# Layer 1 folds along d by a half turn; filter rows by plain loads from SP instead of indirect ones from POOL

## The chip, the cores and the metric

The kernel runs on one core of a Trainium2 chip. The metric is the device time of one execution in microseconds (us). Engines are named as the profile names them: PE (matmuls), PEld (its weight loads), DVE, ACT, POOL, SP. SP, ACT and POOL issue DMAs, which 16 DMA engines carry out.

## What is computed

Four blocks on x of 2048 rows (s) by 448 columns (d), bf16: a spectral filter, an FFN, and both again with the same weights.

```python
def _A_ref(x, w_r, w_i):                       # spectral filter
    X = rfft2(x.astype(float32), axes=(-2, -1))
    X = X * (w_r + 1j * w_i)                   # filter W: 2048 x 225
    return irfft2(X, s=(S, D)).astype(bfloat16)

def _B_ref(x, w1, b1, w2, b2):                 # FFN, 448 -> 1792 -> 448
    r = relu(x @ w1 + b1)
    return (r * r) @ w2 + b2

x = x + _A_ref(_layernorm(x), A_w_r, A_w_i)
x = x + _B_ref(_layernorm(x), B_w1, B_b1, B_w2, B_b2)
x = x + _A_ref(_layernorm(x), A_w_r, A_w_i)
x = x + _B_ref(_layernorm(x), B_w1, B_b1, B_w2, B_b2)
```

## The kernel before

Row s = 16p + t of x lies on partition p, tile t, so x is 16 tiles of 128 x 448. The Fourier transform along s is split into a part over p (128 points, matmuls with the matrix FA) and a part over t (16 points, matrices G and G0); the transform along d is the matrix TD. In layer 1 the stages follow each other like this.

*First stage (`first_A`, line 890).* For each tile t: mean and standard deviation (`ln_stats` on DVE, or `act_stats` on ACT for tiles 1, 3 and 5), their reciprocal (line 885), then `scaled` (lines 756 to 764) multiplies FA by it into `Fs`. Five matmuls per tile use x as the stationary operand and Fs as the moving one. They fold d as they go: the sum and the difference of x at d and at 447 - d come out, which are the cosine and the sine half. The mirrored upper half must lie in memory in mirrored order, so nine copies `XR` (lines 836 to 840) write it into `xr`, a view of `VT`. The fifth matmul takes off the mean. The result is copied out of PSUM into `XA`.

*TD (`stage_TD`, line 924).* 16 steps of four matmuls, each 224 columns, and the copy out (`TD_out`) into `U`. Layer 2 folds twice and uses `TQ` with eight smaller matmuls per pair of steps and a copy that interleaves even and odd frequencies.

*B, W, Bi (lines 952 to 1010).* B does the 16-point transform with G; the result goes to `EF`. `stage_W` (line 981, the operation at line 984, recorded at line 778) multiplies by the filter on DVE: one multiply per n, 128 partitions x 896 elements, which reads through `W_at` (line 797) column block n of the first two blocks of `Wt` and column block 15 - n of the last two. `stage_Bi` brings the product back with H. Then TI and FI (lines 1012 and 1034) finish the inverse transform, and the FFN follows.

*The filter rows in `Wt`.* Partition 32j + 16r + k holds 16 consecutive rows of the filter, 7200 bytes, twice (r = 0, 1). Blocks 0 and 1 are the real and the imaginary part of rows 128k + 16j + 1 and on, blocks 2 and 3 those of the rows counted from the end. Four indirect DMAs on POOL (`gather`, line 825) fetch them with the index table `ix`. Row 0 takes the place of one row that does not exist; two small loads on SP (line 1338) write it over the gathered data, and wait for it.

*Order and waits.* The program is a list of operations with their dependences. `_pages` names the memory pieces that an operation reads and writes. `_Sched.schedule` places the operations in the order of five lists written out by hand, `ORDER`, one for each engine; its times are a model which decides about waits' positions, PSUM banks and the warm-up matmuls on `ones` (line 1364) that fill gaps of PE. Each engine runs its list in order, and an operation that waits holds up all that stand behind it. DMAs of SP go out in the list's order too. In the list of before, SP issues x (alternating with ACT), FA third, `ix`, TD, G, G0, then H (which waits for a reciprocal of the first stage, line 1335), row 0 of the filter, TI, FI, J, biases, W1, TQ, W2.

Of the kernel before, what the change touches and what calls it, by code (L numbers as in the profile page):

```python
# [9 lines left out]
U32 = mybir.dt.uint32  # L10

P = 128
S = 2048
# [20 lines left out]
def make_constants():  # L34
# [21 lines left out]
    l = np.arange(1, 225)[None, :]  # L56
    th = 2 * np.pi * l * (dd - 223.5) / D
    TD = np.zeros((2, 2, P, LW))
    for g, M in enumerate((np.cos(th), -np.sin(th))):
        TD[g, 0] = M[:P]  # L60
        TD[g, 1, 32:] = M[P:]
# [58 lines left out]
    p = np.arange(P)  # L120
    j, k = p // 32, p % 16
    ix = np.stack([P * k + 16 * j + 1, P * (16 - k) - 16 * j - 16], 1)


# [8 lines left out]
    return dict(FA=np.concatenate([FA, -FA], 1), FI=np.concatenate([FI, -FI], 1), TD=TD, G=G, H=H, G0=G0, TI=TI, TQ=TQ, ix=ix,  # L133
# [17 lines left out]
1270 1275 1236 1242 1280 1283 1286 1289 1292""",  # L151
    "act": """
# [11 lines left out]
1035 1172 1184 1177 1174 1179 1182 1253 1246 1248 1251 1256 1261 1268 1278 1266 1263 1271 1258 1273 1276""",  # L164
    "dve": """
# [22 lines left out]
1281 1243 1287 1290 1293""",  # L188
    "pool": """
16 24 25 17 41 23 27 29 81 26 28 22 30 104 21 31 20 32 143 146 18 19""",  # L190
    "sp": """
3 5 6 8 9 11 13 15 33 34 35 150 151 152 153 154 155 156 157 158 159 160 161 162 163 281 301 319 322 321 339 357 375
393 943 964 982 984 985 1002 1020 1038 1150 1056 1147 1188 1144 1194 1241 1191 1235 1285 1238 1141 1282 1244 1288 1197
1291 1294""",
# [10 lines left out]
HALVES = True  # L205
LATE = (4, 4)
# [71 lines left out]
def _pages(ap):  # L278

    if isinstance(ap, _PsAP):  # L280
        return [ap.tile]
    pat = list(ap.ap)
    row = pat[0][0]
    name = ap.tensor.name
    off = np.array([ap.offset % row if row else ap.offset])
    for step, cnt in pat[1:]:
        off = (off[:, None] + step * np.arange(cnt)[None, :]).reshape(-1)
    pg = np.unique(off * mybir.dt.size(ap.dtype) // 4)
    return [(name, int(i)) for i in pg]


class _Sched:
# [6 lines left out]
    DMA_FIRST = 3500.0  # L299
# [76 lines left out]
    def schedule(self):  # L376
# [55 lines left out]
        def ready_of(u):  # L432
            if u not in ready:
                r, off = 0.0, 0.0
                for op in u.ops:
                    for d in op.gdeps:
                        if d.unit is not u:
                            same = d.eng == u.eng and not d.is_dma
                            r = max(r, done[d] + d.lat + (40.0 if u.eng == "pe" else 0.0) - off)
                    off += op.cost  # L440
                ready[u] = r
            return ready[u]
# [34 lines left out]
        while total:  # L477
# [83 lines left out]
            for op in u.ops:  # L561
# [3 lines left out]
                if op.is_dma:  # L565
                    dma_free = max(dma_free, t + 1800.0) + op.lat
                    done[op] = dma_free
# [54 lines left out]
def bass_interleave_layers__spectral_gfnet__dense_activation_squared_relu__prompt_kernel(nc, A_x, A_w_r, A_w_i, B_x, B_w1, B_b1, B_w2, B_b2, out):  # L622
# [3 lines left out]
    dc = {k: nc.inline_tensor(_bf16_round(v), name=f"c_{k}").ap().bitcast(BF16) for k, v in cst.items() if k != "ix"}  # L626
# [829 lines left out]
```

## Time and profile before

| | us |
|---|---|
| median of 3 runs (lowest, highest) | 256.54 (256.44, 257.36) |
| span of the profiled execution | 254.8 |
| PE busy in the span | 246.0 (97%) |
| DVE, ACT, POOL busy | 193.3, 166.5, 12.5 |

One execution was profiled; its span runs from the first to the last instruction, and the median time is 1.7 us longer. Matmuls are pipelined, so a busy PE is not PE at its peak. The page has the span in 40 slices of 6.37 us, busy shares in tenths (9 is 90% or more), the clock granted to TensorE in tenths of full speed, the busy share of the DMA engines, and GB/s:

```profile
PE   6899979999999999999999999999999999999996
DVE  2995988889872899997999998999993078320543
ACT  5896988994287894026847898999449783006600
POOL 3880000000000000000000000000000000000000
PEclk9999999999999999999999999999999999999999
DMA  6999954212111000130000000021223001142004
GB/s 191 380 329 379 293 154 131 42 43 45 36 41 44 0 4 0 41 42 3 0 3 1 3 3 3 3 41 45 46 77 40 0 3 27 37 92 73 3 0 145
```

The DMA engines are busy for the first five or six slices and nearly idle afterwards; POOL works in the first three only.

### The profile page before, as it was taken

The page shows a single profiled execution, that of the slowest core. Times are in us where ns is not written, and L with a number is a line of the kernel's source. Part 1 is how long each engine was busy: PE and PEld are TensorE (multiplying, and loading weights), DVE is VectorE, ACT ScalarE, POOL GpSimd, SP SyncE. Part 2 cuts the span into 40 slices and gives each one's busy share as a digit, 9 for nine tenths or more (in the row PEclk, how much of TensorE's full clock was granted, in tenths as well). Part 3 has the DMA queues.
Part 4 walks back from the last instruction along what each step waited for, and adds up shares of the span by engine and source line. Part 5 has one row for each costly group of instructions (what it writes and reads, how often), then busy time and mean ns, then how long its engine had stood idle before and what let it go on. Part 6 is the DMA issues. An engine that isn't in the chain of part 4 may idle for free.

```text
span 254.8 us, 6150 instructions
## 1 busy us (share of the span) xinstructions
PE 246.0 (97%) x2462; PEld 153.9 (60%) x2462; DVE 193.3 (76%) x628; ACT 166.5 (65%) x362; POOL 12.5 (5%) x26
## 2 busy tenths in 40 slices
PE   6899979999999999999999999999999999999996
PEld 2578777886544555554566688798544445545454
DVE  2995988889872899997999998999993078320543
ACT  5896988994287894026847898999449783006600
POOL 3880000000000000000000000000000000000000
PEclk9999999999999999999999999999999999999999
DMA  6999954212111000130000000021223001142004
GB/s 191 380 329 379 293 154 131 42 43 45 36 41 44 0 4 0 41 42 3 0 3 1 3 3 3 3 41 45 46 77 40 0 3 27 37 92 73 3 0 145
DMA packets 24080, 18.10 MB, mean 71 GB/s; under 512 B 16082, under 2 KB 22706, under 8 KB 24052
## 3 DMA queue, kind: packets, MB, share of 16 engines
q1 hardware_dynamic: 22756, 13.22, 19.3%
q0 software_dynamic: 576, 3.69, 3.9%
q10 hardware_dynamic: 720, 0.80, 1.0%
q8 instruction: 19, 0.31, 0.5%
q14 instruction: 9, 0.07, 0.1%
HBM read 12.20 MB, written 1.84 MB: 55 GB/s over the span
## 4 chain that ended last, share of the span: by engine, by line
PE 82%; ACT 7%; DVE 4%; DMA 2%; issue 1%; POOL 1%; SPq 0%; DVEq 0%; POOLq 0%
PE ps L724 82%; ACT arena L749 4%; ACT VT L749 2%; DMA FA_sb<-c_FA 2%; ACT wide L749 1%; DVE st L854 1%; DVE Fs L761 1%; DVE XA L750 1%; PE ps L1364 0%; POOL Wt L827 0%; DVE x_sb L1217 0%; POOL Fs L761 0%; SPq L716 0%; POOL VT L750 0%; DVE VT L750 0%
## 5 line engine op out<-in xcount | busy, mean ns | idle before, releaser
L724 PE MATMUL ps<-wide,W_sb 64*128 64x512 bf16 (+1 forms) x770 | 90.0, 347 | 0.0
L724 PE MATMUL ps<-W_sb,arena 128*128 128x448 bf16 (+3 forms) x476 | 86.8, 342 | 0.0
L724 PEld LDWEIGHTS ps<-wide,W_sb 64*128 64x128 bf16 (+1 forms) x770 | 51.3, 95 | 36.1 <-issue 0.7
L743 ACT ACTIVATE arena<-ps,b1col 128x512 bf16<-128x512 f32 x84 | 51.9, 690 | 28.9 <-PE ps L724 28.6
L724 PEld LDWEIGHTS ps<-W_sb,arena 128*128 128x128 bf16 x476 | 45.5, 98 | 38.1 <-issue 0.4
L778 DVE TENSOR_TENSOR arena<-arena 128x512 bf16<-128x512 bf16 (+1 forms) x140 | 44.2, 367 | 29.6 <-ACT arena L743 29.5
L1095 ACT ACTIVATE VT<-x_sb 128x448 bf16<-128x448 bf16 x28 | 16.1, 581 | 13.3 <-DVE x_sb L1071 13.2
L749 ACT ACTIVATE arena<-ps 128x896 bf16<-128x896 f32 (+1 forms) x27 | 20.6, 854 | 3.1 <-PE ps L724 3.1
L743 ACT ACTIVATE mv<-mv,epst 128x1 f32<-128x1 f32 (+1 forms) x45 | 12.8, 297 | 11.8 <-DVE mv L855 8.4
L743 ACT ACTIVATE arena<-ps 128x256 bf16<-128x256 f32 x56 | 17.8, 399 | 0.9 <-PE ps L724 0.7
L778 DVE TENSOR_TENSOR wide<-arena,Wt 128x896 bf16<-128x896 bf16 x32 | 17.8, 623 | 0.4 <-DMA Wt<-in_A_w_r_dram,ix 0.3
L749 ACT ACTIVATE XA<-ps 128x512 bf16<-128x512 f32 (+1 forms) x28 | 15.3, 595 | 3.2 <-PE ps L724 3.2
L724 PE MATMUL ps<-H_sb,wide 64*128 64x128 bf16 x512 | 15.7, 217 | 1.5 <-issue 1.4
L1217 DVE SCALAR_TENSOR_TENSOR x_sb<-ps,mv,xin 128x448 bf16<-128x448 f32 (+2 forms) x13 | 8.0, 644 | 11.7 <-PE ps L724 11.5
L724 PEld LDWEIGHTS ps<-H_sb,wide 64*128 64x128 bf16 x512 | 14.4, 94 | 3.5 <-issue 1.5
L724 PE MATMUL ps<-wide,VT 64*128 64x512 bf16 x42 | 15.8, 377 | 0.0
L749 ACT ACTIVATE wide<-ps 128x896 bf16<-128x896 f32 (+3 forms) x20 | 14.1, 761 | 2.2 <-PE ps L724 2.1
L749 ACT ACTIVATE VT<-ps 128x512 bf16<-128x512 f32 (+1 forms) x16 | 12.5, 857 | 1.2 <-PE ps L724 1.2
L1364 PE MATMUL ps<-ones 128*128 128x512 bf16 (+2 forms) x32 | 9.6, 420 | 2.6 <-DVE mv L855 1.0
L760 ACT ACTIVATE wide<-x_sb,rstd 128x448 bf16<-128x448 bf16 x12 | 7.8, 664 | 6.3 <-DVE mv L787 6.0
L750 DVE CAST arena<-ps 128x448 bf16<-128x448 f32 (+1 forms) x11 | 8.8, 832 | 3.1 <-PE ps L724 3.1
L1071 DVE SCALAR_TENSOR_TENSOR x_sb<-ps,mv,xin 128x448 bf16<-128x448 f32 x16 | 10.4, 680 | 0.8 <-PE ps L724 0.7
(79 smaller groups left out, 275.1 us busy)
## 6 DMA issues: line engine op xcount, KB each, us to landing
out_dram<-x_sb SPq DMA_DIRECT2D x15, 112.0 KB, 1.8
W_sb<-in_B_w_dram SPq DMA_DIRECT2D x1, 1568.0 KB, 7.5
H_sb<-c_H SPq DMA_DIRECT2D x2, 768.0 KB, 9.9
W_sb<-in_B_w_dram SPq DMA_DIRECT2D x1, 1344.0 KB, 10.8
xin<-in_A_x_dram SPq DMA_DIRECT2D x3, 224.0 KB, 5.2
G_sb<-c_G SPq DMA_DIRECT2D x1, 512.0 KB, 6.0
xin<-in_A_x_dram ACTq DMA_DIRECT2D x2, 224.0 KB, 4.8
VT<-in_B_w_dram SPq DMA_DIRECT2D x2, 192.0 KB, 3.1
```

Of the source, the lines that this page charges most:

```text
L724: return sch.add("pe", lambda e: e.matmul(_res(o), lhsT, rhs, start=start, stop=stop, skip_group_check=skip), [lhsT, rhs], [o], cost=cost, ...
L743: sch.add("act", lambda e: e.activation(o, _res(i), func, **kw), rd, [o], cost=c)
L749: op = sch.add(engs[0], lambda e: e.activation(o, _res(i), ACT.Copy) if h[0].eng == "act" else e.tensor_copy(o, _res(i)), [i], [o], cost=c ...
L750: e.tensor_copy(o, _res(i)), [i], [o], cost=c[engs[0]], unit=unit)
L760: op = sch.add(engs[0], lambda e: e.activation(o, i, ACT.Copy, scale=s) if h[0].eng == "act" else e.tensor_scalar(o, i, s, 1.0, op0=ALU.mu ...
L761: e.tensor_scalar(o, i, s, 1.0, op0=ALU.mult, op1=ALU.mult), [i, s], [o], cost=c[engs[0]])
L778: sch.add(eng, lambda e: e.tensor_tensor(o, _res(a), b, op), [a, b], [o], cost=_free(o) / rate + 69.0)
L854: small(lambda e, si=si, xi=xi: e.bn_stats(si, xi), [xi], [si], _free(xi) / 0.96 + 69.0)
L1071: small(lambda e, xx=xx, xi=xi, r=r, m=m: e.scalar_tensor_tensor(out=xx, in0=_res(r), scalar=m, in1=xi, op0=ALU.subtract, op1=ALU.add), [r ...
L1095: op = sch.add("act", lambda e, i=i, o=o, x=x, h=h: e.activation(o, x, ACT.Square, accum_out=sd[:, i, 1:2]) if h[0].eng == "act" else e.sc ...
L1217: small(lambda e: e.scalar_tensor_tensor(out=o, in0=_res(i), scalar=rs[0] if rs else 1.0, in1=xi, op0=ALU.add if t >= 4 and last else ALU. ...
L1364: return lambda e: e.matmul(ps[:, b, 0:n], ones[:], ones[:, None, :].to_broadcast([P, n // P, P]), start=True, stop=True)
```

## The change

Layer 1 now folds along d by a half turn: the sum and the difference of x at d and at d + 224 come out of the first stage. They are the even and the odd frequencies, and each needs cosine and sine, so TD holds both for half of the frequencies. The upper half is read where it lies, and the mirrored copies are gone. TD's matmuls write even and odd frequencies into separate columns of PSUM, and the copy out interleaves them, as in layer 2.

The filter rows come by 16 plain loads on SP, one for each of four blocks and each j: 32 partitions, a source access pattern with a count of 2 at stride 0 outermost, then 16 rows, then 3600 elements. In the last block of partitions of blocks 2 and 3 the load leaves out the first row's place, so that the loads of row 0 touch other bytes. `_pages` tells the quarters of `Wt`'s partitions apart.

FA is the first DMA on ACT's queue; x's tiles 1, 3 and 5 follow there, all other tiles go on SP. H no longer waits for the first stage and stands behind row 0 of the filter. The planner's model of a DMA's time and its price of a scaling on DVE are changed, and the five lists of `ORDER` are new: in them POOL has 14 of the first stage's 16 scalings, before 5.

```diff
-    for g, M in enumerate((np.cos(th), -np.sin(th))):
+    for g in range(2):
+        th = 2 * np.pi * np.arange(2 - g, 226 - g, 2)[None, :] * (dd - 223.5) / D
+        M = np.concatenate([np.cos(th), -np.sin(th)], 1)
         TD[g, 0] = M[:P]
         TD[g, 1, 32:] = M[P:]
...
+XLOADS = ((0, 1, "sp"), (1, 1, "act"), (2, 1, "sp"), (3, 1, "act"), (4, 1, "sp"), (5, 1, "act"), (6, 2, "sp"), (8, 2, "sp"),
+          (10, 2, "sp"), (12, 2, "sp"), (14, 2, "sp"))
...
+    if name == "Wt":
+        p = ap.offset // row
+        return [(name, int(i), q) for q in range(p // 32, (p + pat[0][1] - 1) // 32 + 1) for i in pg]
...
-        for a, n, q in ((0, 1, "sp"), (1, 1, "act"), (2, 1, "sp"), (3, 1, "act"), (4, 1, "sp"), (5, 1, "act"), (6, 2, "sp"),
-                        (8, 2, "act"), (10, 2, "sp"), (12, 2, "act"), (14, 2, "sp")):
+        dma("act", FA_sb[:], dc["FA"])
+        for a, n, q in XLOADS:
             dma(q, xin[:, a:a + n, :], x_dram[:, a:a + n, :])
-            if a == 2:
-                dma("sp", FA_sb[:], dc["FA"])
-            if a == 4:
-                dma("sp", ix[:], dc["ix"])
...
-        def gather(c, w, a, n):
-            o = Wt[:, a:a + n * (LW + 1)]
-            sch.add("pool", lambda e: e.indirect_dma_start(o, None, (A_w_r, A_w_i)[w], bass.IndirectOffsetOnAxis(ix[:, c:c + 1], 0)),
-                    [ix[:, c:c + 1]], [o], is_dma=True, cost=1150.0, lat=160.0 * n)
-
-        sch.bias, sch.tag = PR["M"], "M"
-        for w in range(2):
-            gather(0, w, WS * w, 16)
-        sch.tag = "M2"
-        for w in range(2):
-            gather(1, w, WS * (2 + w), 16)
-        for a in range(0, NT, 2):
-            for b in range(a, a + 2) if a == 0 else (a,):
-                n = 1 if a == 0 else 2
-                sch.bias, sch.tag = PR["A1"] - PR["A1step"] * a / 2, f"XR.{b}"
-                evac(xr[:, b:b + n, :], xin[:, b:b + n, D - 1:HD - 1:-1], EV["XR"])
+        def rows(c, w, j):
+
+            a, R, o = (A_w_r, A_w_i)[w], LW + 1, WS * (2 * c + w)
+            d = R + 1 if c == 1 and j == 3 else 0
+            k = (S - 16 - 16 * j if c else 16 * j + 1) * R + d
+            dma("sp", Wt[32 * j:32 * j + 32, o + d:o + WS],
+                bass.AP(a.tensor, a.offset + k, [[0, 2], [-P * R if c else P * R, 16], [1, WS - d]]))
+
         sch.bias, sch.tag = 0.0, ""
         dma("sp", TD_sb[:], dc["TD"])
-        dma("sp", G_sb[:], dc["G"])
-        dma("sp", G0_sb[:], dc["G0"])
+        for c in range(2):
+            for w in range(2):
+                for j in range(4):
+                    sch.tag = f"M.{c}.{w}.{j}"
+                    rows(c, w, j)
+            sch.tag = ""
+            if c == 0:
+                dma("sp", G_sb[:], dc["G"])
+                dma("sp", G0_sb[:], dc["G0"])
...
-                    mm(o(k), xr[:, t, D0[k]:D0[k] + P], F1, False, False, skip=True, unit=u)
+                    mm(o(k), xin[:, t, HD + D0[k]:HD + D0[k] + P], F1, False, False, skip=True, unit=u)
...
                         if first:
-                            l0, w, m = g * LW, LW, TD_sb[:, g, k, :]
+                            r, m = 1 - g, TD_sb[:, g, k, :].rearrange("p (q i) -> p q i", q=2)
+                            o = t[lambda b, i=i, r=r: ps[:, b + i, :].rearrange("p (q w) -> p q w", q=2)[:, :, r * QD:(r + 1) * QD]]
...
-        for i in range(2):
-            dma("sp", H_sb[:, 8 * i:8 * i + 8], dc["H"][:, 8 * i:8 * i + 8], after=[rstd[:, 10 + 2 * i, 0:1]])
         for w, a in enumerate((A_w_r, A_w_i)):
             sch.tag = f"L.W0.{w}"
             dma("sp", Wt[96:128, WS * (2 + w):WS * (2 + w) + LW + 1],
                 bass.AP(a.tensor, a.offset, [[0, 2], [P * (LW + 1), 16], [1, LW + 1]]))
         sch.tag = ""
+        for i in range(2):
+            dma("sp", H_sb[:, 8 * i:8 * i + 8], dc["H"][:, 8 * i:8 * i + 8])
```

More of the change, by code (lines that the diff above doesn't have):

```diff
@@ L9 @@
 FP32 = mybir.dt.float32
-U32 = mybir.dt.uint32
 P = 128
@@ L55, in make_constants @@
     dd = np.arange(HD)[:, None]
-    l = np.arange(1, 225)[None, :]
-    th = 2 * np.pi * l * (dd - 223.5) / D
     TD = np.zeros((2, 2, P, LW))
-    for g, M in enumerate((np.cos(th), -np.sin(th))):
+    for g in range(2):
+        th = 2 * np.pi * np.arange(2 - g, 226 - g, 2)[None, :] * (dd - 223.5) / D
+        M = np.concatenate([np.cos(th), -np.sin(th)], 1)
         TD[g, 0] = M[:P]
@@ L117, in make_constants @@
     H = H.reshape(P, 16, 2, 3, 64)
-    p = np.arange(P)
-    j, k = p // 32, p % 16
-    ix = np.stack([P * k + 16 * j + 1, P * (16 - k) - 16 * j - 16], 1)
     l0 = np.arange(1, 225)[:, None]
@@ L131, in make_constants @@
             TI[:, r, g] = M[r::2]
-    return dict(FA=np.concatenate([FA, -FA], 1), FI=np.concatenate([FI, -FI], 1), TD=TD, G=G, H=H, G0=G0, TI=TI, TQ=TQ, ix=ix,
+    return dict(FA=np.concatenate([FA, -FA], 1), FI=np.concatenate([FI, -FI], 1), TD=TD, G=G, H=H, G0=G0, TI=TI, TQ=TQ,
                 J=np.eye(P)[::-1])
@@ L141 @@
     "pe": """
[9 rows of a table removed]
-1270 1275 1236 1242 1280 1283 1286 1289 1292""",
-    "act": """
[11 rows of a table removed]
-1035 1172 1184 1177 1174 1179 1182 1253 1246 1248 1251 1256 1261 1268 1278 1266 1263 1271 1258 1273 1276""",
-    "dve": """
[22 rows of a table removed]
-1281 1243 1287 1290 1293""",
[9 rows of a table added]
+1267 1272 1277 1244 1238 1285 1288 1282 1291 1294""",
+    "act": """
[11 rows of a table added]
+1174 1186 1181 1184 1176 1055 1248 1255 1253 1250 1258 1260 1268 1263 1280 1278 1273 1270 1275 1265""",
+    "dve": """
[22 rows of a table added]
+1283 1292 1295""",
     "pool": """
-16 24 25 17 41 23 27 29 81 26 28 22 30 104 21 31 20 32 143 146 18 19""",
+15 59 51 43 93 96 75 67 83 109 18 119 122 145 135 132 17 16""",
     "sp": """
-3 5 6 8 9 11 13 15 33 34 35 150 151 152 153 154 155 156 157 158 159 160 161 162 163 281 301 319 322 321 339 357 375
-393 943 964 982 984 985 1002 1020 1038 1150 1056 1147 1188 1144 1194 1241 1191 1235 1285 1238 1141 1282 1244 1288 1197
-1291 1294""",
+4 6 8 10 11 12 13 14 19 20 21 22 23 24 25 26 27 28 29 30 31 32 33 34 35 36 37 152 153 154 155 156 157 158 159 160
+161 162 163 164 165 283 303 321 324 323 341 359 377 395 945 966 984 986 987 1143 1004 1146 1149 1022 1152 1040 1237
+1243 1193 1058 1196 1199 1190 1240 1287 1284 1246 1290 1293 1296""",
 }
@@ L298 @@
     NDSEM = {"sp": 40, "pool": 8, "act": 5, "pe": 0, "dve": 0}
-    DMA_FIRST = 3500.0
+    DMA_FIRST = 2000.0
+    LAND = 400.0
     TURN = 100.0
@@ L438, in ready_of @@
                             same = d.eng == u.eng and not d.is_dma
-                            r = max(r, done[d] + d.lat + (40.0 if u.eng == "pe" else 0.0) - off)
+                            r = max(r, done[d] + (60.0 if d.is_dma and d.cost != 1000.0 else d.lat) + (40.0 if u.eng == "pe" else 0.0) - off)
                     off += op.cost
@@ L565, in schedule @@
                 if op.is_dma:
-                    dma_free = max(dma_free, t + 1800.0) + op.lat
-                    done[op] = dma_free
+                    if op.cost == 1000.0:
+                        dma_free = done[op] = max(dma_free, t + 1800.0) + op.lat
+                    else:
+                        begin = max(dma_free, t + (450.0 if e == "pool" else 1100.0))
+                        dma_free = begin + op.lat * (1.1 if begin < 3400.0 else 2.0 if begin < 5000.0 else 1.08)
+                        done[op] = dma_free + self.LAND
                 for w in op.takes:
@@ L625, in bass_interleave_layers__spectral_gfnet__dense_activation_squared_relu__prompt_kernel @@
     cst = make_constants()
-    dc = {k: nc.inline_tensor(_bf16_round(v), name=f"c_{k}").ap().bitcast(BF16) for k, v in cst.items() if k != "ix"}
-    dc["ix"] = nc.inline_tensor(cst["ix"].astype(np.uint32), name="c_ix").ap()
+    dc = {k: nc.inline_tensor(_bf16_round(v), name=f"c_{k}").ap().bitcast(BF16) for k, v in cst.items()}
     sch = _Sched()
@@ L653, in bass_interleave_layers__spectral_gfnet__dense_activation_squared_relu__prompt_kernel @@
         VT = sb("VT", [P, 2, 2, NT, P])
-        xr = VT[:].rearrange("p a b t c -> p (a b t c)")[:, 0:NT * HD].rearrange("p (t d) -> p t d", t=NT)
         W1u = VT[:].rearrange("p a b t c -> p (a b) (t c)")
         Wt = sb("Wt", [P, 4 * WS])
-        ix = sb("ix", [P, 2], U32)
         TD_sb = sb("TD_sb", [P, 2, 2, LW])
@@ L757, in scaled @@
             n = _free(o)
-            c = {"act": (n + 112.0) / 1.2 + 93.0, "dve": n / 1.92 + 69.0, "pool": 0.83 * n + 245.0}
+            c = {"act": (n + 112.0) / 1.2 + 93.0, "dve": n / 1.92 + (269.0 if "pool" in engs else 69.0), "pool": 0.83 * n + 245.0}
             h = []
@@ L932, in stage_TD, with TD_out @@
                         if first:
-                            l0, w, m = g * LW, LW, TD_sb[:, g, k, :]
+                            r, m = 1 - g, TD_sb[:, g, k, :].rearrange("p (q i) -> p q i", q=2)
+                            o = t[lambda b, i=i, r=r: ps[:, b + i, :].rearrange("p (q w) -> p q w", q=2)[:, :, r * QD:(r + 1) * QD]]
                         else:
                             r = (1 - k) if g == 0 else k
-                            l0, w, m = g * 256 + r * QD, QD, TQ_sb[:, g, r, :]
-                        mm(t[lambda b, i=i, l0=l0, w=w: ps[:, b + i, l0:l0 + w]], x, m, g == 0 and k == 0, g == 1 and k == 1,
-                           skip=True, unit=u)
-            TD_out(t, n0, n, first, EV["TD"])
-        def TD_out(q, c, n, first, engs):
-            o = U[:, c:c + n, :]
-            if first:
-                src = q[lambda b: ps[:, b:b + n, 0:2 * LW]]
-            else:
-                o = o.rearrange("p c (g i r) -> p (c g) i r", g=2, r=2)
-                src = q[lambda b: ps[:, b:b + n, :].rearrange("p b (g w) -> p (b g) w", g=2)[:, :, 0:LW].rearrange(
-                    "p q (r i) -> p q i r", r=2)]
+                            l0, m = g * 256 + r * QD, TQ_sb[:, g, r, :]
+                            o = t[lambda b, i=i, l0=l0: ps[:, b + i, l0:l0 + QD]]
+                        mm(o, x, m, g == 0 and k == 0, g == 1 and k == 1, skip=True, unit=u)
+            TD_out(t, n0, n, EV["TD"])
+        def TD_out(q, c, n, engs):
+            o = U[:, c:c + n, :].rearrange("p c (g i r) -> p (c g) i r", g=2, r=2)
+            src = q[lambda b: ps[:, b:b + n, :].rearrange("p b (g w) -> p (b g) w", g=2)[:, :, 0:LW].rearrange(
+                "p q (r i) -> p q i r", r=2)]
             evac(o, src, engs)
```

84 rows, old and new, of the table ORDER are left out of this document.

## The prediction

> **What bounds the kernel now.** I read the page's totals first, then the chain that ended last, the timeline of the first 40 us, and the views of the DMAs.
>
> ```profile
> span 254.8 us, 6150 instructions
> PE 82%; ACT 7%; DVE 4%; DMA 2%; issue 1%; POOL 1%; SPq 0%; DVEq 0%; POOLq 0%
> q1 hardware_dynamic: 22756, 13.22, 19.3%
> q0 software_dynamic: 576, 3.69, 3.9%
> ```
>
> TensorE carries 82% of the chain, so a stage in which it is never idle cannot be shortened by this change. What the change touches lies ahead of 39 us: the first forward stage, the TD matmuls, and the data of the multiply by the filter W (line 984). Queue q0 is the four indirect gathers of the filter rows: 3.69 MB. The timeline shows how the front of the kernel hangs together (start, duration, engine, instruction; in brackets the idle time before it and its releaser).
>
> ```profile
> 1.65 0.43 SPq L716 DMA_DIRECT2D FA_sb<-c_FA  x1
> 3.29 0.63 DVE L854 BATCH_NORM_STATS2 st<-xin 128x6 f32<-128x448 bf16 x1 [2.40 <-DMA xin<-in_A_x_dram]
> 6.31 0.48 POOL L761 TENSOR_SCALAR Fs<-FA_sb,rstd 128x256 bf16<-128x256 bf16 x1 [1.52 <-DMA FA_sb<-c_FA]
> 10.31 0.28 PE L724 MATMUL ps<-Fs,xin 128*128 128x256 bf16 x1 [0.63 <-POOL Fs L761]
> 16.45 2.98 ACT L749 ACTIVATE XA<-ps 128x512 bf16<-128x512 f32 x6
> 19.36 3.99 PE L724 MATMUL ps<-TD_sb,XA 128*128 128x224 bf16 x40 [0.35 <-DVE XA L750]
> 24.87 1.35 DVE L778 TENSOR_TENSOR wide<-arena,Wt 128x896 bf16<-128x896 bf16 x2 [0.34 <-DMA Wt<-in_A_w_r_dram,ix]
> 27.68 7.08 DVE L778 TENSOR_TENSOR wide<-arena,Wt 128x896 bf16<-128x896 bf16 x13
> 28.60 1.96 PE L724 MATMUL ps<-H_sb,wide 64*128 64x128 bf16 x64
> 39.02 1.32 PE L724 MATMUL ps<-TI_sb,VT 112*128 112x224 bf16 x16 [0.33 <-DVE VT L750]
> ```
>
> Three things to see. FA, issued third on SP, holds the first scaled factor until 6.31. The first stage then runs almost without a gap on PE from 10.31 to 19.36. And the first filter multiply at 24.87 already waits 0.34 us for the filter rows: **the gathers land just in time, with no slack**. The 16 multiplies feed the inverse matmuls (28.60), these the TI stage (39.02). So whatever moves the landing of the *last* filter row moves the rest of the kernel, one for one: each multiply reads all 128 partitions of four blocks of Wt, whichever column it takes.
>
> **The change part by part.**
>
> *FA first, half turn, new order (the first stage).* The mirrored copies go, all on POOL, and the gathers' issues, too:
>
> ```profile
> L750 POOL COPY VT<-xin 128x448 bf16<-128x448 bf16 x7 | 3.8, 556 | 0.0
> L827 POOL DMA_INDIRECT Wt<-in_A_w_i_dram,ix x2 | 2.2, 1088 | 0.9 <-DMA ix<-c_ix 0.8 <-issue 0.2
> L761 POOL TENSOR_SCALAR Fs<-FA_sb,rstd 128x256 bf16<-128x256 bf16 x5 | 2.4, 476 | 1.8 <-DMA FA_sb<-c_FA 1.5 <-DVE rstd L885 0.3
> L749 ACT ACTIVATE XA<-ps 128x512 bf16<-128x512 f32 x12 | 6.7, 597 | 0.0
> ```
>
> POOL gives back 3.8 us of copies (and two small ones) and four issues of about 1 us, and takes 14 of the 16 scalings instead of 5: 14 x 0.476 = 6.7 us, about what it gives back. FA, ahead on ACT's queue, should land with the first x tile (3.29) and no longer at 6.31. PE has the same matmuls. The next limit is ACT: from x's second tile at about 3.7 it has three statistics pairs (some 1.2 us each, 3.6), eleven square roots (2 to 3 us), one scaling (0.5) and 13 copies out of PSUM at 0.50 (2.98 / 6) to 0.60 us, 6.5 to 7.8 us. That is 12.6 to 14.9 us, an end at 16.3 to 18.6 against 19.36: **0.8 to 3.1 us gained, I take 2.5** (it is a chain that mostly runs back to back). Bounds: nothing, and 3.1.
>
> *TD with the half turn.* Even and odd frequencies now come from separate sums; 64 matmuls of 224 columns stay 64 of 224. The copies out of PSUM now interleave, as layer 2 already does. In layer 1 and in layer 2 (two windows of the groups) a copy takes the same:
>
> ```profile
> L749 ACT ACTIVATE arena<-ps 128x896 bf16<-128x896 f32 x10 | 8.7, 936 | 2.2 <-PE ps L724 2.2
> L749 ACT ACTIVATE arena<-ps 128x896 bf16<-128x896 f32 x11 | 9.7, 938 | 0.8 <-PE ps L724 0.8
> ```
>
> Cost: 0.
>
> *Filter rows by 16 plain loads on SP.* They carry the same 3.69 MB as the gathers, in pieces of 7200 bytes: 32 partitions each, whose source access begins with a count of 2 at stride 0 (two copies), then 16 rows. They stand in SP's queue behind x and TD; G and G0 stand between the eighth and the ninth; then come H, TI, FI, the FFN weights. What matters is how many of the 16 DMA engines such a load uses. The kernel before has two loads of exactly this form, the ones of row 0 (line 1338: 32 partitions, source [0,2] outermost). The issue view lists:
>
> ```profile
> H_sb<-c_H SPq DMA_DIRECT2D x2, 768.0 KB, 9.9
> TI_sb<-c_TI SPq DMA_DIRECT2D x1, 196.0 KB, 9.6
> J_sb<-c_J SPq DMA_DIRECT2D x1, 32.0 KB, 8.8
> Wt<-in_A_w_r_dram SPq DMA_DIRECT2D x1, 14.1 KB
> Wt<-in_A_w_i_dram SPq DMA_DIRECT2D x1, 14.1 KB
> b1in<-in_B_b_dram SPq DMA_DIRECT2D x1, 3.5 KB
> W_sb<-in_B_b_dram SPq DMA_DIRECT2D x1, 7.0 KB
> ```
>
> The last figure is the time to landing. The four without one are the loads whose outer count is 2, 2, 14 and 2; those whose count is a multiple of 16 have one (a last store apart). I read it as landing marks from fewer than 16 engines. That the count is then 2 engines, and for each load the same two, is my inference: the trace does not show it outright. The bounds are far apart. Speed per engine:
>
> ```profile
> 2.00:4.00 2.00, 2.00 (x7) 0.71 (x5) 0.63 (x1) 1.36 (x2) 0.68 (x3) 1.00 0.95 266
> 4.00:6.00 2.00, 0.98 (x6) 0.29 (x3) 1.11 (x7) 2.00 (x9) 0.79 (x2) 1.00 0.91 268
> 6.00:8.00 2.00, 1.31 (x8) 0.52 (x7) 1.53 (x3) 1.83 (x8) 0.91 (x2) 1.00 1.04 361
> 8.00:10.00 2.00, 1.68 (x8) 0.51 (x6) 2.00 (x10) 1.93 (x7) 1.98 (x4) 1.00 1.04 411
> 10.00:12.00 2.00, 1.69 (x16) 1.52 (x17) 2.00 (x16) 1.50 (x5) 1.84 (x4) 1.00 1.06 415
> ```
>
> (Windows of 2 us; the last column is GB/s.) At 415 GB/s an engine moves 25.9 GB/s. All 16: 3.69 MB take 8.9 us. Two: 3.69 / 0.0519 = 71 us; by q0's own engine time, 3.9% of 16 x 254.8 us = 159 us, half of it, 79.5 us, with the waits of a full machine in it. I take two engines, the nearest rows being those of the same form, and 71 us, since the other engines are then idle.
>
> [...]
>
> *The sum.* Ahead of the rows stand x (1.835 MB), FA (0.066), TD (0.229): 2.13 MB. The windows give 0.53 + 0.54 + 0.72 = 1.79 MB by 8.0 us, the rest at 411 GB/s: 8.8 us. G and G0, 0.59 MB over 16 engines, add 0.037 MB / 25.9 GB/s = 1.4 us on the two. 8.8 + 71.2 + 1.4 = **81.4 us for the last filter row**. The first multiply was at 24.87: +56.5 us. The 2.5 us gained in the first stage vanish in that wait (cover: none needed, the wait is ten times longer). Behind the waiting multiply in DVE's queue are the other multiplies and some copies of TD and B; PE waits for both, ACT for PE.
>
> H comes behind the rows: 1.57 MB, 3.8 us on each engine, after 0.6 us of row 0, so its two halves land at 83.9 and 85.8. In the kernel before the first inverse matmul came 28.60 - 24.87 = 3.7 us after the first multiply, here at 85.1: the wait for H adds 0 to 1 us, I take 0. After some 35 us of idling PE restarts at a low clock, I expect; the kernel's own start shows the price:
>
> ```profile
> 0.99 3.87 PE L1364 MATMUL ps<-ones 128*128 128x512 bf16 x11 [0.99 <-POOL ones L791]
> 7.68 2.00 PE L1364 MATMUL ps<-ones 128*128 128x512 bf16 x8
> ```
>
> At first 0.35 us a matmul, later 0.25 or less. For some 3 us of inverse matmuls that is 0 to 3 us; I take 1. The FFN weights follow at once (about 91 us and 96 us) and are needed 20 us after the multiplies: 0.
>
> Sum: 56.5 + 0 + 1 = +57.5. The profiled execution spans 254.8 us, and the median of the runs is 1.7 us above it (start and end lie around the span): 254.8 + 57.5 + 1.7 = **314.0 us**.
>
> **The rivals.** *A, the other side: the loads spread over all engines, or over a different pair each.* Then 2.13 + 3.69 + 0.59 MB at 380 to 415 GB/s land by about 20 us, before the multiply that is due at 24.87 - 2.5 = 22.4, and the first stage's gain comes through: 256.5 - 2.5 = **254.0 us**, faster. It decides from the point where the last row lands before 22.4 us: more than about ten engines' worth. For it: x, H, G, all loaded by SP, go at full speed. Against: their outer count is 128. *B, the loads spread but come late*: sixteen issues at 0.43 to 0.83 us, and G in between, delay the last row past 24.87 by 0 to 3 us: 256 to 260, **258 us**. *C, dearer engines*: two engines at the price of 79.5 us: 314.0 + 8.3 = **322 us**; in the range of my case.
>
> **How the numbers follow.** My case 0.90, A 0.07, B 0.03. Range of my case: low by a tenth off the 71 us (the DMA share reads up to 1.06 in these rows, so packets overlap) and 3 us of the later stage regained, since TD and B are done during the wait: 314.0 - 7 - 3 = 304; high by 8.3 and 2 more of the clock: 324. That leaves out A, B and a tenth of my own case, under 2 in 10. Half a per cent, about 1.3 us, is what a measurement of this kernel can tell: A gives faster 0.05 and same 0.02, B same 0.01 and slower 0.02, mine slower 0.90.
>
> **What would show it.** Right: the filter rows' multiply idle for over 50 us on a DMA of Wt, first multiply near 81 us; between 10 and 80 us a DMA share near 0.12 and about 52 GB/s; G's landing near 46 us, so that PE stops after TD until then; PEclk below 1 for a while. The span after the TI stage is unchanged (254.8 - 39.0 = 216 us). The first stage ends near 17 us. Wrong: full GB/s in the first 20 us and the first multiply near 22 us. If the first multiply sits between, the loads use four to eight engines, and my count of two was the faulty step.

## The result, and the profile after

The kernel after takes 317.86 us (median of four runs, 317.62 to 318.28), the kernel before on the same chip 256.9 us (256.44 to 257.36): a ratio of 1.237, 95% interval 1.234 to 1.239. The prediction was 314.0 us in a range of 304 to 324. Medians and ratios here leave out executions more than 1.5% above the fastest of their kernel: two of `before_fa_first` (261.06 and 263.0 us) and the profiled one of `rows_interleaved` (902.16 us).

Of the page of the kernel after, in its order: the span; the busy tenths of PE, the granted clock, the DMA share and GB/s in 40 slices of 7.9 us; and the engines' shares of the chain that ended last.

```profile
span 315.9 us, 6142 instructions
PE   5970018000099999999999999999999999999997
PEclk9895557655569999999999999999999999999999
DMA  7213111137636112210011000000105310131002
GB/s 239 82 54 117 52 53 53 53 94 192 188 96 218 20 30 56 62 36 0 2 33 35 2 0 2 3 2 2 31 6 67 110 48 2 28 85 44 0 17 73
PE 59%; SPq 20%; DMA 7%; DVE 7%; ACT 5%; issue 1%; DVEq 0%
```

PE has two holes in the first eleven slices, and its clock falls to half of full speed in them; before, it was busy there. The DMA engines, before at 90% and more in slices two to five, are about a tenth busy at 52 to 54 GB/s for long stretches. From the twelfth slice on PE is full, as before. 27% of the chain is now SP's queue and DMAs.

The timeline says which instruction opens each hole (start, duration, engine, instruction; in brackets the idle time before it and its releaser):

```profile
0.73 3.72 SPq L717 DMA_DIRECT2D xin<-in_A_x_dram  x8
6.22 0.63 DVE L850 BATCH_NORM_STATS2 st<-xin 128x6 f32<-128x448 bf16 x1 [1.37 <-DMA xin<-in_A_x_dram]
7.16 1.39 POOL L762 TENSOR_SCALAR Fs<-FA_sb,rstd 128x256 bf16<-128x256 bf16 x3 [6.23 <-DVE m L864]
18.93 3.15 PE L725 MATMUL ps<-TD_sb,XA 128*128 128x224 bf16 x31 [0.24 <-DVE XA L751]
41.45 14.96 SPq L717 DMA_DIRECT2D Wt<-in_A_w_i_dram  x4
46.03 0.37 PE L725 MATMUL ps<-TD_sb,XA 128*128 128x224 bf16 x1 [23.95 <-DMA G_sb<-c_G]
64.66 6.03 SPq L717 DMA_DIRECT2D H_sb<-c_H  x2
84.17 2.78 DVE L779 TENSOR_TENSOR wide<-arena,Wt 128x896 bf16<-128x896 bf16 x5 [34.93 <-DMA Wt<-in_A_w_i_dram]
86.60 0.58 PE L725 MATMUL ps<-arena,G_sb 64*64 64x448 bf16 x2 [32.43 <-DMA H_sb<-c_H]
99.30 1.32 PE L725 MATMUL ps<-TI_sb,VT 112*128 112x224 bf16 x16 [0.27 <-DVE VT L751]
```

PE stops after the first TD tiles until G is there at 46.03, does the rest of TD and most of B, and stops again. The first filter multiply comes at 84.17, where it was at 24.87. Between the profiled executions lie 315.9 - 254.8 = 61.1 us: 59.3 up to this multiply, 1.0 from there to the TI stage (99.30 - 84.17 = 15.13, before 14.15), and 0.8 behind it (216.6 us after 215.8). The wait of B and the inverse matmuls for H ends at 86.60, 2.4 us after the first multiply, and the chain that ended last runs through H. Against the kernel before it does not show: the first inverse matmul follows the first multiply by 2.94 us (87.11 after 84.17), before by 3.73 (28.60 after 24.87).

The windows of the wait (busy time of each engine, clock, DMA share, GB/s), and the issue view (KB each, microseconds to landing):

```profile
10.00:20.00 10.00, 9.76 (x91) 8.41 (x90) 7.43 (x31) 8.37 (x22) 6.23 (x14) 0.97 0.13 53
30.00:40.00 10.00, 0.00 (x0) 0.00 (x0) 0.00 (x0) 0.00 (x0) 0.00 (x0) 0.50 0.13 53
70.00:80.00 10.00, 0.00 (x0) 0.00 (x0) 0.00 (x0) 0.00 (x0) 0.00 (x0) 0.50 0.75 191
```

```profile
Wt<-in_A_w_r_dram SPq DMA_DIRECT2D x7, 225.0 KB
G_sb<-c_G SPq DMA_DIRECT2D x1, 512.0 KB, 31.6
H_sb<-c_H SPq DMA_DIRECT2D x2, 768.0 KB, 21.5
FA_sb<-c_FA ACTq DMA_DIRECT2D x1, 64.0 KB, 2.2
```

A share of 0.13 is 2 of 16 engines, and it stays there whether PE works (10 to 20) or stands (30 to 40). The row loads have no landing time, as the four suspicious loads of the kernel before had none.

### The profile page after: what moved, and what is told of

Its sections match the earlier page's. It is cut to its first block, busy times and chain, and to the rows that moved or that the text cites. A ratio compares the mean times of both kernels' runs of the same rounds, so it can differ in the third digit from the quotient of the medians.

```text
span 315.9 us, 6142 instructions
## 1 busy us (share of the span) xinstructions
PE 251.5 (80%) x2459; PEld 160.5 (51%) x2459; DVE 191.2 (61%) x622; ACT 167.3 (53%) x359; POOL 8.0 (3%) x22
## 3 DMA queue, kind: packets, MB, share of 16 engines
HBM read 12.17 MB, written 1.84 MB: 44 GB/s over the span
## 4 chain that ended last, share of the span: by engine, by line
PE 59%; SPq 20%; DMA 7%; DVE 7%; ACT 5%; issue 1%; DVEq 0%
PE ps L725 59%; SPq L717 20%; DMA H_sb<-c_H 7%; ACT arena L750 3%; ACT VT L750 2%; DVE x_sb L1064 1%; DVE wide L779 1%; ACT arena L744 1%; DVE x_sb L1210 1%; DVE st L850 1%; DVE wide L751 1%; DVE Fs L762 0%; DVE VT L1089 0%; PE ps L1357 0%; DVE xin L779 0%
## 5 line engine op out<-in xcount | busy, mean ns | idle before, releaser
L725 PEld LDWEIGHTS ps<-wide,W_sb 64*128 64x128 bf16 (+1 forms) x770 | 53.1, 95 | 31.9 <-ACT arena L744 2.3
L779 DVE TENSOR_TENSOR arena<-arena 128x512 bf16<-128x512 bf16 (+1 forms) x140 | 45.2, 361 | 31.9 <-ACT arena L744 31.8
L725 PE MATMUL ps<-arena,G_sb 64*64 64x448 bf16 (+1 forms) x132 | 10.3, 423 | 32.4 <-DMA H_sb<-c_H 32.4
L725 PE MATMUL ps<-TD_sb,XA 128*128 128x224 bf16 x64 | 8.1, 292 | 24.2 <-DMA G_sb<-c_G 24.0
L751 DVE CAST arena<-ps 128x448 bf16<-128x448 f32 (+1 forms) x13 | 9.9, 796 | 27.9 <-PE ps L725 27.9
L725 PEld LDWEIGHTS ps<-arena,G_sb 64*64 64x64 bf16 x132 | 4.1, 122 | 35.4 <-DMA H_sb<-c_H 32.9
L725 PEld LDWEIGHTS ps<-TD_sb,XA 128*128 128x128 bf16 x64 | 6.8, 110 | 25.8 <-DMA G_sb<-c_G 24.2
L725 PE MATMUL ps<-H_sb,wide 64*128 64x128 bf16 x512 | 17.3, 229 | 0.2
L725 PEld LDWEIGHTS ps<-H_sb,wide 64*128 64x128 bf16 x512 | 15.9, 101 | 2.9 <-issue 1.3
L761 ACT ACTIVATE wide<-x_sb,rstd 128x448 bf16<-128x448 bf16 x14 | 9.2, 670 | 11.9 <-DMA wide<-wide 8.0
```

Source lines behind the costliest of these rows:

```text
L725: return sch.add("pe", lambda e: e.matmul(_res(o), lhsT, rhs, start=start, stop=stop, skip_group_check=skip), [lhsT, rhs], [o], cost=cost, ...
L751: e.tensor_copy(o, _res(i)), [i], [o], cost=c[engs[0]], unit=unit)
L761: op = sch.add(engs[0], lambda e: e.activation(o, i, ACT.Copy, scale=s) if h[0].eng == "act" else e.tensor_scalar(o, i, s, 1.0, op0=ALU.mu ...
L779: sch.add(eng, lambda e: e.tensor_tensor(o, _res(a), b, op), [a, b], [o], cost=_free(o) / rate + 69.0)
```

## The experiments

**Theory:** the count of 2 that stands outermost in the source confines each row load to two engines, and nothing else in the change costs. **Rivals:** the double reading (stride 0) costs; narrow loads of 32 partitions are slow by themselves; G's place between the rows costs; another part of the change costs something.

*Each row load cut in two* (`split16`). Source outermost 16, destination 16 partitions, 32 loads. The blocks 2 and 3 are read in rising order of the rows, so other rows stand in them.

```diff
-            dma("sp", Wt[32 * j:32 * j + 32, o + d:o + WS],
-                bass.AP(a.tensor, a.offset + k, [[0, 2], [-P * R if c else P * R, 16], [1, WS - d]]))
+            u = sch.new_unit("sp")
+            if c == 1:
+                k -= 15 * P * R
+            for r in range(2):
+                dma("sp", Wt[32 * j + 16 * r:32 * j + 16 * r + 16, o + d:o + WS],
+                    bass.AP(a.tensor, a.offset + k, [[P * R, 16], [1, WS - d]]), unit=u)
```

> Each row load is cut into two loads of 16 partitions, so the source begins with a count of 16 and not 2; bytes and pieces are the same (32 loads, 7200-byte pieces). Blocks 2 and 3 take their rows in rising order, so their filter rows are in the wrong order. Engine-count theory: all 16 DMA engines work, the rows move at over 300 GB/s, the last lands at 20 to 25 us, the first multiply stands at 22 to 26 us, time 253 to 259 us. Rival (the pieces, the double reading of each row or the narrow destination are slow, whatever the count): first multiply still past 75 us, time 310 us or more.

It took 262.24 us, ratio 1.021 (1.015 to 1.026). The timeline and two windows of this kernel:

```profile
17.31 3.14 PE L725 MATMUL ps<-TD_sb,XA 128*128 128x224 bf16 x31 [0.24 <-DVE XA L751]
30.66 2.78 DVE L779 TENSOR_TENSOR wide<-arena,Wt 128x896 bf16<-128x896 bf16 x5 [6.15 <-DMA Wt<-in_A_w_i_dram]
```

```profile
10.00:12.00 2.00, 2.00 (x21) 1.79 (x20) 2.00 (x12) 1.97 (x5) 1.56 (x4) 1.00 1.05 213
12.00:14.00 2.00, 2.00 (x21) 1.77 (x19) 1.72 (x10) 2.00 (x7) 1.69 (x5) 1.00 1.01 205
```

The mechanism holds: all engines are busy, and 53.5 of the 59.3 us are gone. The size does not: the multiply was expected at 22 to 26 and stands at 30.66, because the engines move 205 to 213 GB/s, half of the 411 to 415 that the x loads reached. The first stage ends 2.05 us earlier than before (19.36 to 17.31).

Its issue view agrees with how the prediction read a missing landing time. The cut loads, of the same rows and from the same queue, have one; the load of row 0, whose count is still 2, has none:

```profile
Wt<-in_A_w_r_dram SPq DMA_DIRECT2D x14, 112.5 KB, 8.0
Wt<-in_A_w_r_dram SPq DMA_DIRECT2D x1, 14.1 KB
```

A missing time is a sign of few engines and no proof of them, though: in `half_turn_alone` three x tiles of 224 KB and G have none either, with the DMA engines at 90% and more, and the same loads have 5.2 and 6.0 us in the kernel before.

*Only the blocks 0 and 1 cut* (`split_c0`): eight loads of two engines are left.

> Only the eight loads of blocks 0 and 1 are cut into loads of 16 partitions; blocks 2 and 3 keep the source with a count of 2. Engine-count theory: half of the bytes remain for two engines, 1.84 MB at 52 to 54 GB/s, 34 to 35 us; the first multiply moves from 84.2 to 48 to 52 us, time 281 to 287 us. Rival (slowness that is not by bytes on two engines, such as a blocked SP queue): the first multiply stays near 84 us or falls to under 30.

One run, 290.33 us. Timeline and windows:

```profile
58.58 2.78 DVE L779 TENSOR_TENSOR wide<-arena,Wt 128x896 bf16<-128x896 bf16 x5 [35.55 <-DMA Wt<-in_A_w_i_dram]
```

```profile
12.00:14.00 2.00, 2.00 (x21) 1.76 (x19) 1.96 (x10) 2.00 (x6) 1.45 (x4) 1.00 1.02 213
30.00:40.00 10.00, 0.00 (x0) 0.00 (x0) 0.00 (x0) 0.00 (x0) 0.00 (x0) 0.50 0.13 53
```

Half of the two-engine loads leaves about half of the loss (33.7 of 59.3 us at the first multiply). It came 6.6 to 10.6 us later than expected; some 4 us of that are the cut half itself (1.84 MB at 213 instead of 415 GB/s, 8.7 instead of 4.4 us). The rest lies in the last stretch: in the trace's DMA records a packet of 7200 bytes takes 0.27 us from 20 to 43 us, and 0.45 (median) from 44 to 54, when H's packets run beside the rows.

*The second copy from other rows* (`stride_not_zero`). The count 2 stays, its step becomes 16 rows: nothing is read twice, and one copy in two holds other rows.

```diff
-                bass.AP(a.tensor, a.offset + k, [[0, 2], [-P * R if c else P * R, 16], [1, WS - d]]))
+                bass.AP(a.tensor, a.offset + k, [[16 * R, 2], [-P * R if c else P * R, 16], [1, WS - d]]))
```

For the blocks 2 and 3 `k` also begins 16 rows earlier, which these lines do not show.

> The outer count of 2 stays, but its step is 16 rows and not 0, so no row is read twice; half of the partitions hold other rows than they should. Engine-count theory: nothing changes, first multiply at 83 to 85 us, time 316 to 320 us. Rival (two engines reading the same bytes at the same time are what is slow): rows land sooner, time under 300 us.

One run, 319.15 us:

```profile
85.96 2.78 DVE L779 TENSOR_TENSOR wide<-arena,Wt 128x896 bf16<-128x896 bf16 x5 [34.79 <-DMA Wt<-in_A_w_i_dram]
```

The first multiply is as late as with the step 0, so the double reading is not what costs.

*G and G0 ahead of all rows* (`g_first`), by the order of SP's list alone.

> The changed kernel with G and G0 issued ahead of all row loads and not between the eighth and the ninth. Theory (only the last filter row counts): G lands near 11 us instead of 46, TD and B are done by 30 us, and nothing is gained, since the last row lands as before: first multiply at 83 to 85 us, time 315.5 to 319 us. Rival (the 24 us that PE waits for G cost something of their own): time under 312 us.

One run, 318.16 us, first multiply at 84.97. G's wait of 23.95 us, the largest of PE's first hole, costs nothing: whoever fills it still waits for the last row.

*Counts 4 and 16 at 128 partitions* (`outer4_128`, `outer16_128`). These two part the count from the width. Four loads of 128 partitions instead of sixteen of 32; other filter rows are read, and the two loads of row 0 are left out.

```diff
-            dma("sp", Wt[32 * j:32 * j + 32, o + d:o + WS],
-                bass.AP(a.tensor, a.offset + k, [[0, 2], [-P * R if c else P * R, 16], [1, WS - d]]))
+            d = 0
+            k = (64 if c else 1) * R
+            dma("sp", Wt[:, o:o + WS], bass.AP(a.tensor, a.offset + k, [[16 * R, 4], [60 * R, 32], [1, WS]]))
```

With the count 16 the pattern is `[[P * R, 16], [12 * R, 8], [1, WS]]`, and `k` begins at 20 or 1 rows.

> Four loads of 128 partitions instead of sixteen of 32: source outermost count 4, then 32 rows, none read twice, same bytes and pieces of 7200 bytes, other rows of the filter; row 0 is left out. If the outermost count sets the number of engines: 4 engines at 25.9 GB/s, 8.8 + 35.6 + 0.7 = 45.1 us for the last row by the prediction's sum, up to 48 at the rate that the two engines really showed; first multiply 45 to 49, DMA share near 0.25 and some 100 to 108 GB/s between 20 and 40 us; time 277 to 282 us. If instead the loads are slow because they write few partitions (32), 128 partitions bring the full rate: first multiply 22 to 25, 254 to 257 us.

> As the kernel with count 4, but source outermost count 16, then 8 rows: 128 partitions a load, same bytes, other rows, row 0 left out. If the 205 to 213 GB/s of the 16-partition loads came from their few partitions: 128-partition loads move 400 to 415 GB/s, rows land by about 19 to 20 us, the first multiply stands at 22 to 23.5 without a wait, time 253.5 to 256 us (this is the prediction's rival A, and the rest of the change measured with its cover on). If the price lies in the pieces or in a step between them whatever the width: 205 GB/s, rows by 28 to 30, first multiply near 30, 260 to 263 us.

Count 4: 288.42 us, ratio 1.123 (1.119 to 1.127). Count 16: 262.84 us, ratio 1.020 (1.014 to 1.026). Count 4, a window and the timeline:

```profile
14.00:16.00 2.00, 2.00 (x21) 1.77 (x19) 0.95 (x6) 1.53 (x5) 1.92 (x5) 1.00 0.25 79
```

```profile
55.27 2.78 DVE L779 TENSOR_TENSOR wide<-arena,Wt 128x896 bf16<-128x896 bf16 x5 [19.30 <-DMA Wt<-in_A_w_i_dram]
```

Count 16, the same two views:

```profile
12.00:14.00 2.00, 2.00 (x21) 1.76 (x20) 1.97 (x9) 2.00 (x7) 1.38 (x5) 1.00 1.02 227
```

```profile
30.80 2.78 DVE L779 TENSOR_TENSOR wide<-arena,Wt 128x896 bf16<-128x896 bf16 x5 [6.16 <-DMA Wt<-in_A_w_i_dram]
```

DMA shares of 0.13, 0.25 and 1.02 for the outermost counts 2, 4 and 16 are 2, 4 and 16 of 16 engines: in these loads the count is the number of engines. The count 2 was run at 32 partitions, 4 at 128, and 16 at 16, at 128 and (in `rows_interleaved` below) at 32.

Count 4 missed its time: the multiply at 55.27, not 45 to 49, with 79 GB/s at first and 108 later (26 to 28 us) where 104 were expected; and from 30 to 35 us, with H's packets beside them (DMA share 1.01), a row's packet took 0.47 us and not 0.27. And 128 partitions do not bring the full rate: 227 GB/s at count 16. So neither the 32 partitions nor the number of loads (32, or 4) halves the rate.

*Gathers again, and mixtures* (`gathers_back`, `rows_c0_gathers_c1`, `rows_interleaved`). The first keeps all of the change but the row loads: four gathers on POOL, placed by hand between its scalings. The second takes cut loads for the blocks 0 and 1 and gathers for 2 and 3. The third is the second with partition 32j + 2k + r instead of 32j + 16r + k, so that one load of 32 partitions has the source `[[P * R, 16], [0, 2], [1, WS]]`; G, G0 and H are permuted to match.

```diff
+            sch.add("pool", lambda e: e.indirect_dma_start(o, None, (A_w_r, A_w_i)[w], bass.IndirectOffsetOnAxis(ix[:, c:c + 1], 0)),
+                    [ix[:, c:c + 1]], [o], is_dma=True, cost=1150.0, lat=160.0 * 16)
```

> The change without its row loads: the four indirect gathers are back on POOL, two after the third scaling, one after the eighth and one after the ninth; FA first, half turn and the new order stay. If the row loads are the whole loss: time 254 to 259 us, first multiply at 23 to 27 us. Rival (the new order or the half turn costs something of its own): above 262 us.

> Blocks 0 and 1 by loads of 16 partitions with a count of 16, blocks 2 and 3 by two indirect gathers on POOL, after the third and the eighth scaling; H stands ahead of row 0 of the filter. Theory: at the 205 GB/s that the loads of 16 partitions reached and with the gathers beside them all rows land by 20 to 23 us, the first stage ends near 18 us, first multiply at 23 to 25 us, time 254.5 to 257.5 us. If the narrow loads also hold up the gathers: 258 us or more.

> As rows_c0_gathers_c1, but the two copies of a row stand side by side (partition 32j + 2k + r; G, G0 and H are permuted to fit), so that a load of 32 partitions has the count of 16 outermost and the step 0 inside. Engine-count theory: 16 engines, and if the narrow destination is what halved the rate, 32 partitions give over 300 GB/s; the loads of blocks 0 and 1 are done by 14 us, first multiply at 22 to 24.5 us, time 253.5 to 256.5 us. If the step 0 or the 32 partitions are slow in themselves: no faster than rows_c0_gathers_c1.

They took 261.54 us (1.017, 1.009 to 1.025), 264.82 us (1.030, 1.024 to 1.037) and 265.55 us (1.031, 1.024 to 1.038). With the gathers back, the multiply at 28.63 waits for no filter row; what is late there is the first stage (TD starts at 23.40). The gathers' issues stand between POOL's scalings (1.01 us of issuing before the last five). And one scaling on DVE takes 3.85 us, in the kernel after 0.56, while POOL works without a gap from 14.24 to 18.75; PE waits 1.70 us for the copy behind it. Why DVE takes so long there isn't shown. That placement is the experiment's own, so this run shows that the loss of 60 us goes with the row loads, and no more. The timeline of the first:

```profile
14.98 3.85 DVE L762 TENSOR_SCALAR Fs<-FA_sb,rstd 128x256 bf16<-128x256 bf16 x1 [0.34 <-PE ps L725]
23.40 3.23 PE L725 MATMUL ps<-TD_sb,XA 128*128 128x224 bf16 x32 [0.33 <-DVE XA L751]
28.63 2.77 DVE L779 TENSOR_TENSOR wide<-arena,Wt 128x896 bf16<-128x896 bf16 x5
```

Both mixtures missed what was hoped of them (254.5 to 257.5 and 253.5 to 256.5 us). In the second, cut loads and gathers share busy engines (DMA share 1.03 at 198 GB/s from 12 to 14 us). The trace of the third is of the execution at 902 us, in which PE's matmuls took about 1 us each instead of 0.35, for a reason that isn't known; so only its DMA rows are read: from 10 to 12 us, with no gather begun, the loads of 32 partitions kept all engines busy (share 1.03) at 231 GB/s. Neither mixture beats the gathers alone.

*The other parts alone* (`before_fa_first`, `half_turn_alone`, `half_turn_fa_first`): on the kernel before, with its gathers and its order, FA as the first DMA on ACT; the half turn; both.

```diff
-                dma("sp", FA_sb[:], dc["FA"])
+                dma("act", FA_sb[:], dc["FA"])
```

> The kernel before with one thing changed: FA is the first DMA on ACT's queue instead of the third on SP's. FA lands near 3 us instead of 6.2. If FA held up the first stage: its matmuls start up to 0.7 us earlier and the time falls by 0.3 to 0.7 us. If x's later tiles or POOL set the pace anyway: within 0.3 us of the kernel before.

> The kernel before with the half turn only: no mirrored copies, the new TD and its copy out, gathers on POOL and all else in the old order. The prediction costs TD at 0 and the first stage is bound on ACT and by FA's landing, not by POOL's copies: PE's first stage ends within 0.5 us of 19.36, time 256 to 257.5, no difference. Rival: the copies did hold the gathers on POOL, and these now go out earlier, so the 0.34 us of wait goes: up to 0.5 us faster. A second rival: the interleaving copy or the strided PSUM writes of the matmuls cost: slower by 1 us or more.

> The half turn, and FA as the first DMA on ACT's queue, gathers and old order else. FA first alone measured no difference on the kernel before. If the first stage is bound on ACT: 256 to 257.5, no difference. If both together free it (the first factor early, and no copy between the scalings on POOL): TD starts 1 to 2 us before 19.36, the first multiply then waits on the gathers unless these went out earlier too: 254.5 to 256.

FA first: 257.96 us, ratio 1.002 (0.998 to 1.006). Half turn: 256.07 us, ratio 0.995 (0.993 to 0.998). Both: 257.5 us, ratio 1.002 (1.000 to 1.004). The half turn alone is the one version that comes out ahead of the kernel before, by about the 0.5% that can be told from no change. Its timeline:

```profile
18.07 3.99 PE L724 MATMUL ps<-TD_sb,XA 128*128 128x224 bf16 x40 [0.33 <-DVE XA L750]
25.82 1.17 DVE L778 TENSOR_TENSOR wide<-arena,Wt 128x896 bf16<-128x896 bf16 x2 [2.58 <-DMA Wt<-in_A_w_r_dram,ix]
38.64 1.32 PE L724 MATMUL ps<-TI_sb,VT 112*128 112x224 bf16 x16 [0.32 <-DVE VT L750]
```

TD starts 1.29 us earlier than before, which was not expected (within 0.5 us of 19.36): the copies on POOL did hold the stage, for all but the 0.33 us by which FA landed earlier (first factor at 5.98, before at 6.31). But the multiply waits 2.58 us for the gathers and comes at 25.82, later even than 24.87; the just-in-time landing that the prediction read is the next bound. With TD and B further on by then, the TI stage still starts 0.38 us earlier (39.02 to 38.64), which is the span's gain (254.8 to 254.4). These are single executions, and those of the kernel before beside this run spread over 2 us (256.19 to 258.33), so the ratio is the firmer figure. And with FA first besides:

```profile
6.27 0.58 ACT L871 ACTIVATE wide<-xin 128x448 bf16<-128x448 bf16 x1 [1.11 <-DMA xin<-in_A_x_dram]
7.50 0.48 POOL L761 TENSOR_SCALAR Fs<-FA_sb,rstd 128x256 bf16<-128x256 bf16 x1 [5.77 <-DVE m L863]
19.48 3.99 PE L724 MATMUL ps<-TD_sb,XA 128*128 128x224 bf16 x40 [0.33 <-DVE XA L750]
```

The first factor waits for statistics now and not for FA, and it is 1.5 us later than with the half turn alone, not earlier: FA ahead on ACT's queue puts ACT's x tiles behind it, ACT waits 1.11 us for one of them before its second statistics, and DVE's reciprocal stands in the list behind a square root of ACT. In this execution it takes back what the half turn gave (TD at 19.48).

## Why the prediction was right, step by step

- **Two engines: right, and shown.** The share of 0.13, the dose (half of the loads, about half of the loss), the step without double reading, the shares at counts 4 and 16, and, as a sign only, the landing times that the cut loads have and the loads with count 2 and 4 lack.
- **The first multiply at 81.4: 2.8 us short** (84.17). The rate in the windows to 40 us is what was taken (53 against 51.9 GB/s). Two terms are missing from the sum, and the trace's DMA records part them. First, "the other engines are then idle" does not hold to the end: H's packets begin at 69.28 us, and beside them (share 0.75 at 191 GB/s from 70 to 80) a row's packet takes 0.47 us (median, 69.3 to 76) instead of 0.27, and the rows' rate falls from 53 to 32 GB/s. The last row's packet ends at 83.43, 2.0 us after the sum; at 53 GB/s to the end it would have been about 79.2 (an estimate from the 0.53 MB left at 69.3). Second, the loads of row 0 stand behind the last row and write bytes that the multiply reads, too. The sum has their 0.6 us ahead of H, but not ahead of the multiply; their packets end at 84.16, 0.7 us after the last row's.
- **H at no cost and the clock at 1 us: 1.0 together**, as predicted, but in part by luck. The clock did fall to 0.50, and against the kernel before the way from the first multiply to TI grew by 1.0 us (15.13 after 14.15). Against `split16`, which has the same order of work and a granted clock of 1.00 there, it grew by 2.4 (12.70, from 30.66 to 43.36): the first inverse matmul comes 0.9 us later behind the multiply (2.94 after 2.06), and the first 64 of them take 3.59 us instead of 1.96. So H and the clock cost more than was taken, and some 1.4 us came back, probably since TD and B were done during the wait, which the prediction had in its lower bound only. The span behind TI grew by 0.8, which was taken as unchanged. With 59.3 instead of 56.5 these make 61.1 instead of 57.5. The inverse matmuls of the kernel after, then of `split16`:

```profile
87.11 3.59 PE L725 MATMUL ps<-H_sb,wide 64*128 64x128 bf16 x64
32.72 1.96 PE L725 MATMUL ps<-H_sb,wide 64*128 64x128 bf16 x64 [0.44 <-DMA H_sb<-c_H]
```

- **2.5 us of the first stage: only 0.4** in the kernel after (18.93). Mis-sized in the step "FA should land with the first x tile": it did (2.2 us from its issue), but the first factor then waits for the statistics and comes at 7.16, where the step had x at 3.29 as the start. DVE stands 1.37 us before 6.22 for an x tile. And the clock, which the step did not have, fell already here: four matmuls of the second tile took 1.06 us, later 0.60. In `split16`, with a first factor at 6.28 and a clock of 1.00, the stage ends at 17.31, near the predicted 17; that is 2.05 us of the gain. In the kernel after all this is hidden in the long wait. The window of the clock:

```profile
8.00:10.00 2.00, 2.00 (x11) 1.29 (x10) 2.00 (x10) 1.72 (x7) 0.55 (x2) 0.50 0.40 153
```

- **G at 46:** it was 46.03. What the sum hadn't is SP's own queue: issues of row loads took up to 8.6 us each, and H was issued only at 64.66; its wait ended at 86.60, where the sum had 85.8. That the late issue changed nothing, since the two engines were the bound, is argued and was not tried apart.
- **Rival A was priced wrongly.** Loads spread over 16 engines were put at 380 to 415 GB/s and 254 us, faster than before. Spread, as 16, 32 or 128 partitions a load, they run at 205 to 231 GB/s, and the two kernels with such loads alone take 262 to 263 us: no row load tried here beats the gathers. A window of the kernel before shows the gathers at work on the same rows and pieces:

```profile
14.00:16.00 2.00, 2.00 (x21) 1.74 (x19) 2.00 (x10) 1.83 (x5) 1.82 (x3) 1.00 0.97 403
```

A packet of 7200 bytes took 0.27 us in this window and 0.50 to 0.55 in the spread loads (10 to 12 or 16 us). Why these loads run at half the rate **stays open**; the pieces and the width are out, and so are the rows, where the same ones are read (`split16` for the blocks 0 and 1). No row load with 128 outermost was run.

## What to carry to other kernels

Look at the outermost count in the source of every DMA that the critical path waits for: the repeat count of 2 there took 14 of 16 engines away here (share 0.13 at 53 GB/s), and the profile of a kernel that already has one such load can point at the form by a missing landing time (a last store lacks it, too, and in some runs here full loads did, so check the count). Ask also what runs beside such a load towards its end. A share near 1 isn't yet a full rate (1.05 came with 213 GB/s in `split16`, 1.06 with 415 in the kernel before): read GB/s beside it, and compare with another load of the same bytes. An earlier first stage is worth only what the next arrival leaves: here 1.29 us at TD's start were 0.38 us at the TI stage, since the multiply between them waits for the gathers.

## What the hardware showed unexpectedly

- Loads on all 16 engines at a share of 1.0 moved 205 to 231 GB/s, others 400 to 415; two engines alone, with the same pieces of 7200 bytes, moved 53 GB/s, 26 GB/s each (415 on all 16 is 25.9 each).
- Loads on two or four engines slowed down beside H's loads (share 0.75 in the kernel after, 1.01 in `outer4_128`): a row's packet of 7200 bytes took 0.27 us alone and 0.45 to 0.48 us (medians) with H's packets beside it, in the kernel after, `split_c0`, `stride_not_zero` and `outer4_128`.
- SP's issues took long while earlier loads held two engines: 14.96 us for four row loads, where SP needed 3.72 us for the eight x loads and 3.67 for eight cut row loads in `split16` (from 13.54 us). H, beside whose packets the share rose to 0.75 (70 to 80 us), was issued at 64.66 only, though the share had been 0.13 from 50 to 60 us.
- The granted clock was 0.50 not only while PE stood but also in the first work after each wait. Two windows of the kernel after, with 3.97 and 3.40 us of PE work in them:

```profile
40.00:50.00 10.00, 3.97 (x35) 2.40 (x36) 1.15 (x2) 2.74 (x3) 0.00 (x0) 0.50 0.13 53
86.00:90.00 4.00, 3.40 (x58) 3.02 (x60) 4.00 (x7) 1.88 (x2) 0.00 (x0) 0.50 0.70 231
```
